# Threshold attention and a feed-forward layer on one core: v in wide packets, another key order, another order of work

## The chip, the cores and the metric

The kernel runs on one core of a Trainium2 chip. The metric is the time of one execution in device microseconds (us); less is better. A core has engines that each run their own list of instructions in order and wait for each other by semaphores: TensorE (PE in the profile, its weight loads PEld), VectorE (DVE), ScalarE (ACT), GpSimd (POOL) and SyncE (SP). SP only issues DMAs here; POOL issues DMAs and adds tensors. All DMAs run on the same 16 DMA engines.

## The reference

Eight batches of eight heads of attention over 576 positions with 64 dimensions per head, in which only scores within tau of their row's maximum count, and then a feed-forward layer with 512 model and 2048 hidden dimensions:

```
scores = (1/sqrt(64)) * q @ k.T
thresh = max(scores, axis=-1) - tau
scores = where(scores >= thresh, scores, -1e9)
scores = scores - max(scores, axis=-1)
attn   = exp(scores) / (sum(exp(scores)) + 1e-9)
x      = (attn @ v), heads side by side      # 4608 x 512
h      = x @ w_in
out    = (h * sigmoid(1.702 * h)) @ w_out
```

q, k and v are float32. The weights w_in and w_out come as float64, 16 pieces of 128 x 512 each, and the kernel turns them into float32 by operations on their bits.

## The kernel before

**Attention.** The work unit is a pair of heads; there are 32 pairs (n = 0 to 31), four per batch. A pair's keys are cut into nine tiles of 64. For every pair:

- `load_qk` (L366) and `load_v` (L377) issue the loads on SP, four DMAs for each of q, k and v; k of pair 0 alone goes by ACT's queue. q and k come in runs of 32 floats (128 B), v in runs of 64 (256 B). v stands twice in SBUF, once in each half of the partitions. Key number 64j + r lies in tile j, row r.
- `prep` (L477, VectorE) transposes q and k in blocks of 32; `scores` (L493, TensorE) makes the nine tiles of scores in PSUM; `keep` (L510, ACT) copies them to SBUF.
- `in_groups` (L516), `over_tiles` (L525), `over_halves` (L536, L542) and `turn_rows` (L553), all VectorE, find every query's maximum less the gap that tau gives. `row_out` (L566) writes this row of thresholds to DRAM and `row_in` (L575) reads it back to all partitions, both on SP. Pair 2 alone does without (`spread_max`, L557).
- `sub` (L580, VectorE) subtracts the row, `mask` (L586, ACT) sends what is below it to a huge negative number, `exps` (L590, ACT) takes exponentials. Each goes in five steps of two tiles, the last of one.
- `values` and `sums_by_pe` (both L601, TensorE; pv and den in the profile) multiply by v and by ones. From pair 5 on the sums are made on VectorE by `in_groups` with addition; pairs 5 to 7 then spread them by `one_group` and `spread_sums` (L643, L647, L684, L686), pairs from 8 on by `turn_sums` (L658 to L663) and a way through DRAM on SP (`sums_out` L668, `sums_in` L675).
- `place_x` (L703, VectorE) scales the product into the tiles xT. It frees the PSUM buffer of the product.

**Weights.** `load_w` (L428, L429, POOL) loads a piece by two DMAs of 512 KB into a staging place (six of them; a place is taken again when its piece is converted); `cv_ex` (L439), `cv_frac` (L453, L457), `cv_end` (L465) on VectorE and `cv_power` (L447) on ACT convert it. The task `hold` (L484, POOL) is a small copy that waits for a prepared k: weight loads 0 to 2 come after the k of pair 2, loads 3 to 5 after the k of pair 3. All later loads stand behind these in POOL's list.

**Feed-forward.** Two blocks of 256 rows are done plainly: `mm1_0` (L758), `tanh`, `gelu_0` (L764), `mm2` (L740), `half` (L747); the first step needs pairs 0 to 3 placed and w_in converted, `mm2` needs w_out converted. The blocks after them use sums of quarters of matrices so that seven products do the work of eight (L718, L909; for the last four blocks L823 too), with `t_minus` (L865, ACT) and `t_plus` (L869, POOL's DMA) making such sums of w_out once. POOL adds at L875 to L888.

**Start.** POOL sets a few constants (L944 to L947) and loads tau (L948). `tau_terms` (L960 to L969, VectorE) derives the gap from it; it comes after the preparing of pair 0's q and k and pair 1's q, and ahead of pair 1's k.

**What sets the order.** Nothing of this order is written out. The kernel describes each step as a task with an engine, a cost, the tasks it follows, buffers that it takes and gives back, and a rank: the pair's number plus a bias for the kind of step (tables `EARLY` for pairs 0 to 3, `SECOND` for pairs 4 to 7, `LATER`, and `CV` for the weights). `run_in_order` plays an event clock over these tasks while the program is built: whenever an engine is free it takes the ready task of lowest rank, and issues its instructions. So costs, lags (from the end of a task to when another engine may see it) and biases fix each engine's list, and the chip then runs the lists. A load was a task on SP with a fixed lag for its DMA (10.0 for q and k of pairs 4 to 7, 9.0 for a weight piece, 3.0 for v).

Of the kernel before, what the change touches and what calls it, by code (L numbers as in the profile page):

```python
# [19 lines left out]
P = 128  # L20
# [10 lines left out]
def kernel(  # L31
# [84 lines left out]
    stop = const.tile([P, 1], FP32, name="stop")  # L116
    shift = const.tile([P, 1], FP32, name="shift")
# [9 lines left out]
    for x in ("raw0", "raw1", "qkT0", "qkT1", "mb"):  # L127
# [6 lines left out]
        "exps": -11.47,  # L134
        "in_groups": 5.75,
        "keep": 10.66,
        "load_qk": -0.27,
        "load_v": 4.86,
        "mask": -2.66,
        "one_group": -15.86,  # L140
        "one_row": 12.67,
        "over_halves": -7.01,
        "over_tiles": -4.01,
        "place_x": -17.11,
        "prep": -11.73,
        "row_in": 20.49,
        "row_out": 4.47,
        "scores_run": 12.45,
        "spread_max": -1.73,
        "spread_sums": 7.14,  # L150
        "sub": 9.27,
        "sums_by_pe": 0.27,
        "sums_in": -9.39,
        "sums_out": 2.13,
        "turn_rows": -12.55,
        "turn_sums": -0.41,
        "values": 14.64,
        "w_sum": 4.11,
        "x_sum": -14.1,
    }  # L160
    SECOND = {
        "exps": -7.29,
        "in_groups": 20.95,
        "keep": 16.67,
        "load_qk": -8.88,
        "load_v": 5.53,
        "mask": 2.36,
        "one_group": 2.55,
        "one_row": -2.71,
        "over_halves": -12.07,  # L170
        "over_tiles": 2.86,
        "place_x": -20.26,
        "prep": 3.49,
        "row_in": -19.42,
        "row_out": -24.08,
        "scores_run": -7.99,
        "spread_max": -3.11,
        "spread_sums": -2.29,
        "sub": 14.98,
        "sums_by_pe": 35.93,  # L180
        "sums_in": 7.43,
        "sums_out": 4.05,
        "turn_rows": -3.84,
        "turn_sums": 4.03,
        "values": 11.79,
        "w_sum": -10.45,
        "x_sum": -10.98,
    }
    LATER = {
        "exps": 2.01,  # L190
        "in_groups": 10.37,
        "keep": -0.02,
        "load_qk": -6.6,
        "load_v": 3.77,
        "mask": 14.79,
        "one_group": 4.78,
        "one_row": -14.98,
        "over_halves": 1.09,
        "over_tiles": -6.27,
        "place_x": -0.34,  # L200
        "prep": 2.34,
        "row_in": 4.02,
        "row_out": 2.64,
        "scores_run": -11.25,
        "spread_max": -9.44,
        "spread_sums": -6.73,
        "sub": 2.14,
        "sums_by_pe": 1.46,
        "sums_in": 3.78,
        "sums_out": 2.16,  # L210
        "turn_rows": 12.26,
        "turn_sums": 0.29,
        "values": -10.38,
        "w_sum": 6.61,
        "x_sum": 6.02,
    }
    CV = {
        "cv_end": -8.05,
        "cv_ex": 2.22,
        "cv_frac": -11.72,  # L220
        "cv_power": -4.72,
        "load_w": -7.79,
    }

    LAG = {"PE": 0.26, "DVE": 0.18, "ACT": 0.22, "POOL": 0.18}

    QUARTERS = ("scores", "scores_run", "values", "sums_by_pe")
# [12 lines left out]
    FIRST, LAST = -9.0, 1000.0  # L240
    need, follows = {}, {}

    def run_in_order():
# [7 lines left out]
        events = [(0.0, 1, i) for i, n in enumerate(left) if n == 0]  # L251
# [3 lines left out]
        mode, held_for = None, None  # L255
        while events:
            now = events[0][0]
            while events and events[0][0] <= now:
                _, kind, i = heapq.heappop(events)
                engine, _, rank, _, _, _, _, give, lag = tasks[i]  # L260
                if kind == 0:
                    busy.discard(engine)
                    heapq.heappush(events, (now + lag, 2, i))
                elif kind == 1:
                    ready.setdefault(engine, []).append((rank, i))
                else:
                    for pool in give:
                        free[pool] += 1

                for u in users[i]:  # L270
                    if kind == (0 if tasks[u][0] == engine else 2):
                        left[u] -= 1
                        if left[u] == 0:
                            ready.setdefault(tasks[u][0], []).append((tasks[u][2], u))
            for engine, queue in ready.items():
                if engine in busy:
                    continue
                for rank, i in sorted(queue):
# [14 lines left out]
                cost = tasks[i][1]  # L293
                if engine == "PE":
# [3 lines left out]
                heapq.heappush(events, (now + cost, 0, i))  # L298
                started += 1
# [4 lines left out]
    JOINT = 7  # L304

# [53 lines left out]
    def load_qk(n, which, queue):  # L359
# [4 lines left out]
        for h in range(2):  # L364
            for j in range(2):
                queue.dma_start(  # L366
                    out=blocks[ds(64 * h + 32 * j, 32), :, :],
                    in_=src[b, 2 * hp + h, :, ts(j, 32)].rearrange("(c p) d -> p c d", p=32),
# [3 lines left out]
    def load_v(n):  # L372
        b, hp = divmod(n, NPAIR)
        t = seat("v_m", n % 2).rearrange("p (j h d) -> p j h d", j=NK, h=2)
        for h in range(2):
            for c in range(2):
                nc.sync.dma_start(  # L377
                    out=t[ts(c, KT), :, h, :],
                    in_=v[b, 2 * hp + h].rearrange("(j k) d -> k j d", k=KT),
# [109 lines left out]
    def scores(n, j):  # L489
# [8 lines left out]
        if j == NK - 1:  # L498
# [33 lines left out]
    def over_halves(n):  # L532
        r = stats[n, ALU.max]
        o = work.tile([P, QB], FP32, name="fold", tag="fold", bufs=1)
        for x in (1, 3) if n in BY_DMA else range(4):
# [3 lines left out]
            )  # L539
        if n in BY_DMA:  # L540
# [10 lines left out]
    def turn_rows(n):  # L551

        nc.vector.transpose(out=flat[1], in_=flat[0])  # L553

# [23 lines left out]
    def sub(n, t):  # L578
        s = sT[n, t].rearrange("p u h s -> p u (h s)")
        nc.vector.tensor_tensor(  # L580
# [26 lines left out]
    def values(n, tiles):  # L607
# [3 lines left out]
        by_values(n, lambda j, h: v_m[:, j, h, :], [pv[:, c, :] for c in range(2)], tiles)  # L611
        if n < NPAIR:
            free_scores(n, tiles)

    def sums_by_pe(n, tiles, apart):
# [9 lines left out]
        if not apart:  # L625
# [321 lines left out]
    nc.gpsimd.memset(ones, 1.0)  # L947
    nc.gpsimd.dma_start(  # L948
# [26 lines left out]
    BY_PE = 5  # L975
    BY_DMA = (0, 1, *range(3, NP))
    SUMS_BY_DMA = range(8, NP)
    LEAD = 6
    WHOLE = 6

    FFU = 1.727
    T_RANK = FIRST

    W_RANK = (0, 12.87, 12.51, 22.24, 0, 4.97)
    ready_w, w_loads, w64 = [], [], 0
    for i in range(len(pieces)):
# [10 lines left out]
        a = task("POOL", 1.1, rank, load_w, i, after=w_loads[-1:], take=place, lag=9.0)  # L997
        w_loads.append(a)
        e = task("DVE", 0.345, rank, cv_ex, i, after=[a])
        m = task("ACT", 0.67, rank, cv_power, i, after=[e])  # L1000
        a = task("DVE", 1.1, rank, cv_frac, i, after=[e])

        over = [ready_w[y] for y in range(i) if i >= n_in and stage(y) == (i - n_in) // PER_STAGE]
        ready_w.append(task("DVE", 0.61, rank, cv_end, i, after=[a, m] + over, give=place))
# [191 lines left out]
    for n in range(NP):  # L1196
# [5 lines left out]
        slow = 1.1 if n < NPAIR else 1.0  # L1202
# [3 lines left out]
        cost = 3.5 if NPAIR <= n < 2 * NPAIR else 2.0  # L1206
        lag = (4.6, 3.0)[n] if n < 2 else 10.0 if n < 2 * NPAIR else 3.0
        lq = task("SP", cost, r - 2.0, load_qk, n, 0, q0, after=behind, take=own(n, "raw0"), lag=lag)
        lk = task(
            "SP", cost if n else 0.1, r - 2.0, load_qk, n, 1, q1, after=behind,  # L1210
            take=own(n, "raw1"), lag=lag,
        )
        v_m = f"v_m{n % 2}"
        lv = task("SP", 2.4, r + (1.85 if n < 2 else -1.2), load_v, n, after=lvs[-1:], take=(v_m,), lag=3.0)
        lvs.append(lv)
        pq = task("DVE", 0.69, r, prep, n, 0, after=[lq], take=own(n, "qkT0"), give=own(n, "raw0"))
# [3 lines left out]
        if n in (2, 3):  # L1220
# [3 lines left out]
            for a in w_loads[3 * (n - 2) : 3 * (n - 1)]:  # L1224
# [3 lines left out]
        def copied(n, r, j, a):  # L1228
            copies.append(task("ACT", 0.55, r, keep, n, j, after=[a] + copies[-1:], give=("psA",)))
            if j % 2 or j == NK - 1:  # L1230
                mx.append(task(
                    "DVE", 1.27 if j % 2 else 0.66, r, in_groups, n, j // 2, ALU.max,
# [29 lines left out]
        else:  # L1262
            for js in [range(x, x + 3) for x in range(0, NK, 3)] if n >= WHOLE else [[x] for x in range(NK)]:
# [4 lines left out]
                    give=own(n, "qkT0", "qkT1") if js[-1] == NK - 1 else (),  # L1268
# [107 lines left out]
```

## Time and profile before

| what | us |
|---|---|
| median of 3 runs | 1317.7 |
| lowest, highest | 1315.8, 1318.82 |
| the profiled execution | 1317.94 |
| its span, first to last instruction | 1316.2 |
| PE busy in it | 1260.9 |
| DVE busy | 1006.1 |
| ACT busy | 646.6 |
| POOL busy | 249.0 |

The mean granted TensorE clock of the profiled run was 0.987. The profile names instructions by engine and line of the code; in a group's row, `out<-in` are the program's buffers. arena, w_out and w_in are the large SBUF tiles in which most small buffers have seats, so that the line says more than the name. Numbers in brackets at the end of a row in order of time are idle time of the engine before that group and what ended it. The page's slices cut the span into 40 equal parts and give the busy share in tenths.

### The profile page before, as it was taken

Reading aid. Unit: us, or ns where it says so; the run is one execution under the profiler, and the core shown is the slowest. Engines: PE = TensorE matmul, PEld = TensorE weight load, DVE = VectorE, ACT = ScalarE, POOL = GpSimd, SP = SyncE. Lnnn points to the kernel's source line nnn. Section 1 sums busy time; section 2 is a strip of 40 time slices with the busy share of each in tenths; the row PEclk is TensorE's granted clock in tenths of the full one; section 3 lists DMA queues with packets and bytes.
Section 4 is the critical chain, followed back from the end, with each engine's and each line's share of the span. In section 5 each row is a group of like instructions: output and inputs, shape, how many; then the busy total and the mean of one; then the engine's idle time right before and its main releaser. Section 6 shows DMA issues by size and latency. Waiting matters only on the chain. (4 is left out here: it accounts for less than half of the span.)

```text
span 1316.2 us, 22807 instructions
## 1 busy us (share of the span) xinstructions
PE 1260.9 (96%) x9128; PEld 975.6 (74%) x9128; DVE 1006.1 (76%) x1610; ACT 646.6 (49%) x830; POOL 249.0 (19%) x291
## 2 busy tenths in 40 slices
PE   5669999999999999999999999999999999999998
PEld 2346864457887777777778888777777778888887
DVE  7989999898888887788777877777888863652642
ACT  4876666576554555555554555454556540210210
POOL 1201211012031211213021303030212117120120
PEclk8879999999999999999999999999999999999999
DMA  8976766545323223212213222323122110000000
GB/s 152 293 189 207 230 207 149 112 77 100 85 55 71 55 55 71 51 50 54 58 42 72 55 71 55 71 55 71 36 55 54 36 46 8 9 1 25 8 0 32
DMA packets 258819, 102.88 MB, mean 78 GB/s; under 512 B 233754, under 2 KB 243994, under 8 KB 258714
## 3 DMA queue, kind: packets, MB, share of 16 engines
q1 hardware_dynamic: 244986, 63.40, 22.4%
q0 software_dynamic: 11360, 37.74, 9.3%
q8 instruction: 71, 1.16, 0.4%
q10 hardware_dynamic: 2368, 0.30, 0.2%
q14 instruction: 34, 0.28, 0.1%
HBM read 87.51 MB, written 9.69 MB: 74 GB/s over the span
## 5 line engine op out<-in xcount | busy, mean ns | idle before, releaser
L516 DVE TRANSPOSE_TENSOR_REDUCE part<-arena 128x36 f32<-128x1152 f32 (+1 forms) x295 | 357.5, 1235 | 41.9 <-ACT arena L510 32.4
L718 PE MATMUL hps<-xT,w_in 128*128 128x256 f32 x1536 | 337.2, 380 | 0.5 <-DVE arena L730 0.4
L718 PEld LDWEIGHTS hps<-xT,w_in 128*128 128x128 f32 x1536 | 290.7, 190 | 45.9 <-issue 5.7
L586 ACT ACTIVATE arena<-arena 128x1152 f32<-128x1152 f32 (+1 forms) x160 | 169.4, 1059 | 144.0 <-DVE arena L580 143.8
L510 ACT COPY arena<-ps 128x576 f32<-128x576 f32 x288 | 170.7, 647 | 115.3 <-PE ps L493 111.9
L580 DVE TENSOR_TENSOR arena<-arena 128x1152 f32<-128x1152 f32 (+1 forms) x158 | 201.1, 1313 | 20.5 <-DMA arena<-row 20.5
L909 PE MATMUL ops<-w_out,arena 128*128 128x256 f32 x896 | 202.4, 380 | 1.8 <-DVE arena L730 1.8
L590 ACT ACTIVATE arena<-arena,shift,scl 128x1152 f32<-128x1152 f32 (+1 forms) x160 | 200.3, 1252 | 4.1
L493 PE MATMUL ps<-arena 64*64 64x288 f32 x2304 | 174.7, 420 | 22.9 <-DVE arena L477 15.3
L909 PEld LDWEIGHTS ops<-w_out,arena 128*128 128x128 f32 x896 | 169.3, 190 | 28.7 <-DVE arena L730 3.1
L875 POOL TENSOR_TENSOR arena<-arena 128x256 f32<-128x256 f32 x56 | 49.7, 888 | 647.1 <-DVE arena L730 543.9
L601 PE MATMUL pv<-arena 64*64 64x288 f32 x2176 | 159.7, 408 | 0.0
L727 ACT ACTIVATE th<-hps 128x512 f32<-128x512 f32 x112 | 66.0, 589 | 186.0 <-PE hps L718 171.8
L909 PE MATMUL ops<-arena 128*128 128x256 f32 x672 | 150.7, 380 | 0.7 <-DVE osb L931 0.7
L493 PEld LDWEIGHTS ps<-arena 64*64 64x64 f32 x2304 | 84.0, 137 | 90.8 <-ACT arena L510 30.4
L909 PEld LDWEIGHTS ops<-arena 128*128 128x128 f32 x672 | 127.1, 190 | 20.4 <-issue 2.2
L601 PEld LDWEIGHTS pv<-arena 64*64 64x64 f32 x2176 | 82.1, 134 | 54.1 <-issue 10.0
L931 DVE SCALAR_TENSOR_TENSOR osb<-ops,osb 128x256 f32<-128x256 f32 x98 | 39.3, 413 | 97.9 <-PE ops L909 90.6
L730 DVE SCALAR_TENSOR_TENSOR arena<-th,hps 128x512 f32<-128x512 f32 x96 | 64.2, 669 | 46.7 <-ACT th L727 46.4
L740 PE MATMUL ops<-w_out,arena 128*128 128x512 f32 x128 | 57.2, 600 | 3.2 <-DVE w_out L465 2.2
L758 PE MATMUL hps<-xT,w_in 128*128 128x256 f32 x256 | 56.4, 381 | 0.0
L888 POOL TENSOR_TENSOR arena<-arena 128x512 f32<-128x512 f32 x28 | 35.6, 1272 | 108.3 <-PE ops L909 108.3
(115 smaller groups left out, 1044.7 us busy)
## 6 DMA issues: line engine op xcount, KB each, us to landing
arena<-in_v_dram SPq DMA_DIRECT2D x128, 144.0 KB
arena<-in_q_dram SPq DMA_DIRECT2D x128, 72.0 KB
out_dram<-osb SPq DMA_DIRECT2D x36, 256.0 KB
arena<-in_k_dram SPq DMA_DIRECT2D x124, 72.0 KB
arena<-row SPq DMA_DIRECT2D x62, 144.0 KB
arena<-row_s SPq DMA_DIRECT2D x48, 144.0 KB
w_out<-in_moe_w_in_dram POOLq DMA_DIRECT2D x12, 512.0 KB, 9.5
arena<-in_moe_w_out_dram POOLq DMA_DIRECT2D x12, 512.0 KB, 6.3
```

The costliest lines, as they stand in the source:

```text
L493: nc.tensor.matmul(ps[ts(c, KT), h, 0:SH], lhsT=mats[n, 1][ts(h, D), ts(j, KT)], rhs=mats[n, 0][ts(h, D), ts(c, SH)], start=True, stop=True,)
L510: nc.scalar.copy(out=sT[n, t][:, u], in_=pss.pop((n, j))[:, :, 0:SH])
L516: nc.vector.tensor_reduce(out=stats[n, op][:, t * 2 * QB : min(2 * t + 2, NK) * QB], in_=sT[n, t].rearrange("p u h (g d) -> p (u h g) d", ...
L580: nc.vector.tensor_tensor(out=s, in0=s, in1=mbs[n].unsqueeze(1).to_broadcast(list(s.shape)), op=ALU.subtract)
L586: nc.scalar.activation(out=s, in_=s, func=AF.Prelu, alpha=STEEP)
L590: nc.scalar.activation(out=s, in_=s, func=AF.Exp, scale=scl, bias=shift)
L601: nc.tensor.matmul(o[c][ts(h, D), 0:SH], lhsT=left(j, h)[ts(c, KT)], rhs=sT[n, t][ts(c, KT), u, h, :], start=(j == 0), stop=(j == NK - 1),)
L718: nc.tensor.matmul(hidden[j][:, ts(f, BLK)], lhsT=w_in[:, c, ds((f * HF + j) * P, P)], rhs=xTs[blk][:, c, :], start=(c == 0), stop=(c == N ...
L727: nc.scalar.activation(out=ths[j], in_=hidden[j], func=AF.Tanh, scale=GELU_SCALE / 2)
L730: nc.vector.scalar_tensor_tensor(out=g[:, :, j, :], in0=two(ths.pop(j)), scalar=1.0, in1=two(hidden.pop(j)), op0=ALU.add, op1=ALU.mult,)
L740: nc.tensor.matmul(acc[i], lhsT=g0[:, j, ts(i, P)], rhs=w_out[:, j, :], start=(j == 0), stop=(j == NFC - 1),)
L909: nc.tensor.matmul(banks[blk][k][:, ts(o, HM)], lhsT=left[:, j, :], rhs=right[:, j, :], start=(j == 0), stop=(j == HF - 1),)
```

## The change

- **v.** A partition takes nine consecutive keys of a head, 9 x 64 floats in one run of 2304 B; key 9r + j lies in tile j, row r. The k loads are reordered to match: the same 128 B runs from other rows. Where v is used, two indices change places.
- **Planner.** A load becomes two tasks: the issue on its queue (SP or POOL), and a transfer on one of two movers, DMS for SP's loads and DMW for weights. Alone a mover runs at full rate; together SP's transfer gets a share of 0.055 (packets of 128 B) or 0.3 (others), the weights the rest. Costs of SP's issues and of some VectorE and ACT steps have new figures.
- **Biases.** All values of the four tables but one or two and the ranks of the weight pieces (`W_RANK`) change, so the order on every engine does.
- **Weights.** The first six loads all come after the k of pair 3.
- **Sums.** Pairs 5 to 7 turn their sums by DMA too (`SUMS_BY_DMA` from 5 on). The condition under which the seats of the scores are given back is written in terms of the new list `SUMS_BY_PE`.
- **Start.** POOL sets two more constants, `minus` and `own_row`, ahead of tau's load. They serve functions (`row_blocks`, `again`, `mask_one`) for pairs in `TWICE`, and `BY_POOL` would move some subtractions to POOL; both lists are empty, so none of this is issued.

The diff, cut to its core:

```diff
+    minus = const.tile([P, 2, KT], FP32, name="minus")
+    own_row = const.tile([P, QB // 2], FP32, name="own_row")
...
     EARLY = {
-        "exps": -11.47,
-        "in_groups": 5.75,
+        "exps": -17.61,
+        "in_groups": 12.77,
...
+    MOVERS = ("DMS", "DMW")
+    SHARE = (0.055, 0.3)
+    def transfer(by, time, a, kind=0, give=(), lag=1.7):
+        return task(by, time, FIRST, moved, kind, after=[a], give=give, lag=lag)
...
+        def rates():
+            if len(flow) < 2:
+                return dict.fromkeys(flow, 1.0)
+            x = SHARE[tasks[flow["DMS"][0]][4][0]]
+            return {"DMS": x, "DMW": 1.0 - x}
...
+    TWICE = ()
+    BY_POOL = {}
...
+                rows = src[b, 2 * hp + h, :, ts(j, 32)]
                 queue.dma_start(
                     out=blocks[ds(64 * h + 32 * j, 32), :, :],
-                    in_=src[b, 2 * hp + h, :, ts(j, 32)].rearrange("(c p) d -> p c d", p=32),
+                    in_=rows.rearrange("(a p t) d -> p t a d", a=2, p=32) if which
+                    else rows.rearrange("(c p) d -> p c d", p=32),
                 )
...
-        t = seat("v_m", n % 2).rearrange("p (j h d) -> p j h d", j=NK, h=2)
+        t = seat("v_m", n % 2).rearrange("p (h j d) -> p h j d", j=NK, h=2)
         for h in range(2):
             for c in range(2):
                 nc.sync.dma_start(
-                    out=t[ts(c, KT), :, h, :],
-                    in_=v[b, 2 * hp + h].rearrange("(j k) d -> k j d", k=KT),
+                    out=t[ts(c, KT), h],
+                    in_=v[b, 2 * hp + h].rearrange("(k j) d -> k j d", k=KT),
                 )
...
-        by_values(n, lambda j, h: v_m[:, j, h, :], [pv[:, c, :] for c in range(2)], tiles)
+        by_values(n, lambda j, h: v_m[:, h, j, :], [pv[:, c, :] for c in range(2)], tiles)
...
     nc.gpsimd.memset(ones, 1.0)
+    nc.gpsimd.memset(minus, 0.0)
+    nc.gpsimd.memset(own_row, 0.0)
+    for x in range(4):
+        nc.gpsimd.memset(minus[ts(x, 32), x % 2, :], -1.0)
+        nc.gpsimd.affine_select(
+            out=own_row[ts(x, 32)], in_=own_row[ts(x, 32)], compare_op=ALU.not_equal, fill=1.0,
+            base=-(QB // 2) * (x // 2), pattern=[[-1, QB // 2]], channel_multiplier=1,
+        )
     nc.gpsimd.dma_start(
         out=tau_b, in_=bass.AP(tensor=tau.tensor, offset=tau.offset, ap=[[0, P], [1, 1]])
     )
...
-    BY_PE = 5
+    SUMS_BY_PE = (0, 1, 2, 3, 4)
     BY_DMA = (0, 1, *range(3, NP))
-    SUMS_BY_DMA = range(8, NP)
+    SUMS_BY_DMA = range(5, NP)
...
-    W_RANK = (0, 12.87, 12.51, 22.24, 0, 4.97)
+    W_RANK = (0, 15.75, 22.55, 26.06, 2.06, 16.74)
...
-        a = task("POOL", 1.1, rank, load_w, i, after=w_loads[-1:], take=place, lag=9.0)
+        a = task("POOL", 1.1, rank, load_w, i, after=w_loads[-1:], take=place)
         w_loads.append(a)
+        a = transfer("DMW", 3.4, a)
...
-        cost = 3.5 if NPAIR <= n < 2 * NPAIR else 2.0
-        lag = (4.6, 3.0)[n] if n < 2 else 10.0 if n < 2 * NPAIR else 3.0
-        lq = task("SP", cost, r - 2.0, load_qk, n, 0, q0, after=behind, take=own(n, "raw0"), lag=lag)
+        cost = (2.6, 2.4, 2.9, 2.4)[n] if n < NPAIR else 2.1
+        lq = task("SP", cost, r - 2.0, load_qk, n, 0, q0, after=behind, take=own(n, "raw0"))
...
+        lq, lk = (transfer("DMS", 1.45, a, lag=1.7 if n else 3.0) for a in (lq, lk))
...
-        lv = task("SP", 2.4, r + (1.85 if n < 2 else -1.2), load_v, n, after=lvs[-1:], take=(v_m,), lag=3.0)
+        lv = task("SP", 3.0, r + (1.85 if n < 2 else -1.2), load_v, n, after=lvs[-1:], take=(v_m,))
         lvs.append(lv)
+        lv = transfer("DMS", 1.1, lv, 1)
...
-        if n in (2, 3):
+        if n == 3:
             h = task("POOL", 0.3, FIRST, hold, n, after=[pk])
-            for a in w_loads[3 * (n - 2) : 3 * (n - 1)]:
+            for a in w_loads[0:6]:
                 tasks[a][5].append(h)
```

## The prediction

> **What bounds the kernel now.** I read the page's slices first, then busy time in stretches of 10 us, then what VectorE (DVE), TensorE (PE), SyncE (SP) and GpSimd (POOL) did in order of time, with the wait before each group in brackets. The slices:
>
> ```profile
> PE   5669999999999999999999999999999999999998
> DVE  7989999898888887788777877777888863652642
> ```
>
> A slice is 32.9 us. From the fifth on TensorE is full: there the time is its own work, which the change leaves alone (4566 matmuls in both programs). Only its idle time can go: span 1316.2 less 1260.9 busy is 55.3 us. The first 120 us hold 41.2 of them, 180 to 330 us 7.2, and 3.4 lie after the last matmul.
>
> ```profile
> 20.00:30.00 10.00, 4.03 (x40) 2.49 (x44) 9.83 (x16) 2.77 (x6) 3.52 (x8) 0.66 0.72 157
> 70.00:80.00 10.00, 0.76 (x12) 0.21 (x8) 9.80 (x14) 7.05 (x7) 0.00 (x0) 0.69 1.13 316
> 110.00:120.00 10.00, 9.52 (x132) 5.71 (x124) 9.24 (x22) 7.71 (x13) 0.00 (x0) 1.00 0.70 226
> 120.00:130.00 10.00, 10.00 (x51) 8.66 (x47) 9.83 (x13) 3.15 (x5) 3.17 (x6) 1.00 0.57 210
> ```
>
> Third column PE, then weight loads, then DVE: while TensorE has 4.0 or 0.8 of 10 us, VectorE has 9.8. The first 115 us are VectorE's: softmax work of four pairs and the conversion of w_in. TensorE fills up once pair 3 (the fourth) is placed and the feed-forward layer can start:
>
> ```profile
> 9.16 0.11 DVE L960 TENSOR_SCALAR neg<-tau_b 128x1 f32<-128x1 f32 x1
> 34.67 2.63 DVE L580 TENSOR_TENSOR arena<-arena 128x1152 f32<-128x1152 f32 x2 [0.23 <-DMA arena<-row]
> 88.56 2.63 DVE L580 TENSOR_TENSOR arena<-arena 128x1152 f32<-128x1152 f32 x2 [3.70 <-DMA arena<-row]
> 114.40 0.95 DVE L703 TENSOR_TENSOR xT<-pv,arena 128x256 f32<-128x256 f32 x4
> ```
> ```profile
> 117.60 1.99 PE L758 MATMUL hps<-xT,w_in 128*128 128x256 f32 x8
> 215.38 20.01 PE L740 MATMUL ops<-w_out,arena 128*128 128x512 f32 x46 [1.63 <-DVE w_out L465]
> 271.23 1.78 PE L493 MATMUL ps<-arena 64*64 64x288 f32 x16 [2.16 <-ACT arena L510]
> ```
>
> So the time is VectorE's until pair 3 is placed, then TensorE's plus a few waits. The gates: row DMAs, and the two chains that the edits at the start touch:
>
> ```profile
> 26.20 1.13 SPq L575 DMA_DIRECT2D arena<-row  x2
> ```
> ```profile
> 1.39 0.75 POOL L948 DMA_DIRECT2D tau_b<-in_tau_dram  x1 [0.35 <-issue]
> 25.89 0.18 POOL L484 COPY stop<-arena 128x1 f32<-128x1 f32 x1 [23.75 <-DVE arena L477]
> 26.01 0.56 POOL L428 DMA_DIRECT2D w_out<-in_moe_w_in_dram  x1
> ```
> ```profile
> L875 POOLq MODIFY_POOL_CONFIG  x2: 675/675/675, 284.1 to 284.1; - x2
> ```
>
> **What the Trainium skill says.** GPSIMD Engine Reference, 2.1 Instruction dispatch: the first call into a freshly loaded library pays a load of about 6 us (5.95) that the profile doesn't show. Here POOL's first tensor op comes at 290.10, 6.0 after the load instruction at 284.1, but VectorE released it only at 290.02: the trace bounds the price from above, no more. DMA: Bandwidth & Descriptors, Queues, rings and completion order: an engine goes round its queues by whole packets. The trace agrees: between 72 and 73 us, under weight loads, SP's queue moved 88 small packets, between 80 and 81 alone 1140. The same page, Specifications, asks for 512 B or more per transfer: those 1140 packets were 0.14 MB, against 0.42 MB in the weights' microsecond.
>
> **Part by part.** Sums are made against the profiled run (1317.94; span 1316.2 and 1.74 around it); the median of the runs is 1317.7, 0.2 less.
>
> *v in packets of 2304 B, keys reordered.* A pair's v was 2304 packets of 256 B; it becomes 256. At about 1013 packets/us (5066 in 10 to 15 us) 2.3 us of all DMA engines become 0.59 MB at 0.35 MB/us, 1.7. k keeps 128 B packets in another order. No wait on v is in the list of waits, so the path gains nothing: 0, cover being that v comes microseconds ahead of the values matmul. SP's issue of a v load (0.63 each, L377) is between the 0.48 of the like-shaped row load (L575) and the planner's new 0.75: four of them 0.6 less or 0.5 more, beside VectorE work.
>
> *New order up to pair 3.* In the built program I compared VectorE's lists up to the last place_x of pair 3. They hold the same work but for one more cv_end (0.61). Before, that point ended at 115.35. Of the waits between 19.46 (pair 0's row turned) and there, 6.0 in all, the list shows 0.23 and 3.70 on row DMAs, 0.80 on ACT's power, 0.97 on scores that held a transpose's target. The 3.70 came from SP: pair 3's row was ready at 77.8 but sent at 82.19, behind v3, q4 and k4. In the new list q4 and k4 are through by about 66 (v3 waits for pair 1's values at about 59, then 2.7 and 4.3), the row goes at 80.4 on time, and between its turn and its first use VectorE has pair 2's placing and three conversions: 8.6 us, against 7.3 for v4's issue (2.7), row_out (0.7), row_in (1.1) and landing (2.6, from 85.98 to 88.56), and 0.2 between. Also the two q/k prepares stand late enough. So 115.35 + 0.61 - 6.0 = 110.0, plus new waits:
> - Pair 1's row. SP sends it when VectorE has turned it (30.3), takes it in 33.0 to 34.1; before, row 0 issued to 27.3 beside three weight pieces was used at 34.67 (7.3 later). 41.4 against a use at 40.7 to 41.0: 0.4.
> - Conversion power: ACT has pair 4's nine copies ahead of pieces 5 to 7: 0.9.
> - tau, below: 3.0.
>
> Placed at 114.3. Then TensorE has still to end pair 5's scores, which ACT copies at about 0.8 each behind five powers: 1.4 later, 115.7. Before it began at 117.60 with 0.5 of those scores undone, so 118.1. **First part: -2.4.**
>
> *First six loads behind k of pair 3.* They start when that k is prepared: 31.0 by the sum, not 25.9. Queued behind POOL's copy are all loads, nothing else; VectorE's conversions wait for them. Piece 0's second DMA landed about 8.1 after the start (the tenth DMA, waiting for it, went at 34.16): 39.2, use at 39.6. 0, with no margin; in return row 0 travels without weights beside it.
>
> *POOL's added constants.* Two memsets, four pairs of memset and affine_select, and a library load before the first select stand ahead of tau's DMA; behind that DMA wait tau_terms and, in order on VectorE, everything from pair 1's k on. Memsets to 1.5 (0.10 to 0.15 each, 0.74 on), load instruction 0.7, the page's 5.95, seven ops at about 0.15: 9.2; landing 3.9: 13.1. VectorE wanted tau at 9.16 and had 0.94 of waits just after, so 3.0. Low end 0 (load hidden); high end 6 (DMA engines are at 104% between 10 and 15 us). I take 3.0. The rest of these constants feeds branches with empty lists.
>
> *Pairs 5 to 7 turn sums by DMA.* Per pair four fold copies stay; out go 0.69 (L647), 0.27 and 0.78, in come 0.18, 0.27, 0.21: 1.1 less, 3 in all, on a VectorE that TensorE waits for only in the next item; on SP four DMAs more per pair (about 1.9), between 200 and 260 us where it stands waiting anyway. 0 by itself. The freeing of score seats is the same at its moment; the planner's costs act only through the order.
>
> *New order after the start of the feed-forward layer.* Up to the last conversion of w_out VectorE's list holds 183 us of work, before 199 (each kind times its mean): sums and maxima of pairs 5 to 7 now stand behind it. So it ends near 195 where it ended at 215.32, and TensorE needs it near 198. That removes 1.63 and 0.60. The 2.16 before L493 (ACT was in pair 7's exponentials) goes too: pair 7's subtractions are done some 15 us before TensorE gets there. Left are about 0.9 of GELU waits, 0.9 where ACT's two sign copies stand between score copies, 0.5 others: 2.3 of the 7.2. That is 4.9; I take **-3.5**, since the old order met waits too that its list alone doesn't show. After 330 us: 0.
>
> Sum: 1317.9 - 2.4 - 3.5 = **1312.0**.
>
> **Rivals.** *A, as summed:* 1312, own range 1308 to 1315. For it: VectorE's 9.8 of 10. *B, tau isn't late:* the first part is 5.4 and the second up to 4.9: 1317.9 - 9.9 = 1308. For it: the trace never shows the load's price; against: the page. *C, given back:* the second part is spent on waits that the list doesn't show (row 5, q7 under the last loads): 1317.9 - 2.4 + 1 = 1316.5. Speaks for it: q and k crawl under weights (88 against 1140 packets). *D, slower: pair 1's row drowns in six loads released in its own microsecond.* Before, three pieces went ahead; now twelve DMAs of 0.5 MB at 0.35 MB/us flow 17 us, from 35 to 52. If row_in lands only with them, VectorE stands at pair 1's first sub (43.7, tau included) for 8.5 us with everything behind it. 6.1 more than cancel 5.9, and the second part shrinks by half as TensorE catches less: 1312 + 8.5 + 1.8 = 1322. It decides from a wait of 6 us. Against it: round-robin gave row 0 its 0.3 MB in 6.5 us. *That the packets don't do what they say* gives A: nothing waits on v.
>
> **Chances.** A 0.50, B 0.22, C 0.16, D 0.12. Measured apart can be about 0.2%, 2.6 us: faster is below 1315.1. That is nearly all of A (0.49), B, and 0.04 of C: 0.75; same 0.12 of C, 0.01 of A and 0.02 of D: 0.15; slower 0.10. Range 1305 to 1320: it takes in B's low end and C, and leaves out most of D and B with every wait gone.
>
> **What would show it.** Right: tau_terms near 13; L666's first sub on pair 0 near 34, before any conversion; hps begins near 115.7; last L510 near 195; no wait on w_out at ops. Wrong: a wait of several us before pair 1's sub (D), tau near 9 (B), hps no earlier than 117.6 or waits on hps and ps above 7 us between 180 and 330 (C).

## The result and the profile after

| what | before | after |
|---|---|---|
| median, us | 1317.7 | 1312.81 |
| lowest, highest | 1315.8, 1320.58 | 1311.6, 1315.22 |
| profiled execution | 1317.94 | 1311.6 |
| its span | 1316.2 | 1309.8 |
| PE busy in it | 1260.9 | 1260.5 |

The ratio of after to before is 0.9962, with an interval of 0.9948 to 0.9975: 4.9 us faster, against 1312.0 forecast. TensorE's work is as it was; its idle time went from 55.3 to 49.3 us. The profiled execution of after is its quickest, so the two profiles lie 6.3 us apart where the medians lie 4.9 apart.

The page's slices after:

```profile
PE   5869999999999999999999999999999999999998
DVE  7999998989998877778877877777888864652642
```

TensorE's second slice rises from 6 to 8, and its long row of nines stays. Where the idle time went shows in busy time by stretch. The third column is PE, then weight loads, DVE, ACT, POOL, the granted clock, the share of the DMA engines and GB/s. First before, then after:

```profile
0.00:120.00 120.00, 79.00 (x1016) 45.33 (x1016) 103.53 (x179) 87.16 (x110) 18.74 (x43) 0.87 0.81 208
120.00:180.00 60.00, 60.00 (x400) 49.15 (x396) 58.44 (x99) 30.74 (x39) 13.39 (x24) 1.00 0.74 238
180.00:240.00 60.00, 55.91 (x371) 27.75 (x373) 58.34 (x98) 41.12 (x54) 7.42 (x10) 1.00 0.66 151
240.00:330.00 90.00, 86.90 (x697) 54.64 (x690) 80.30 (x120) 60.82 (x77) 13.10 (x14) 0.98 0.49 93
```
```profile
0.00:120.00 120.00, 82.32 (x1036) 46.09 (x1037) 107.88 (x186) 88.57 (x113) 20.89 (x52) 0.90 0.75 208
120.00:180.00 60.00, 58.74 (x381) 47.19 (x383) 56.83 (x102) 28.29 (x38) 15.59 (x28) 1.00 0.84 270
180.00:240.00 60.00, 59.66 (x319) 28.02 (x312) 54.47 (x76) 44.40 (x52) 5.45 (x6) 1.00 0.67 139
240.00:330.00 90.00, 86.17 (x746) 58.12 (x744) 81.66 (x125) 58.64 (x76) 17.87 (x16) 0.98 0.44 90
```

In the first stretch TensorE gains 3.3 us. From 120 to 330 its idle time goes from 7.2 to 5.4 us (1.26 + 0.34 + 3.83): 3.75 better between 180 and 240, but 1.26 and 0.7 given back on either side. After 330 it is 0.9 less: a single wait of 1.42 for a GELU, at 1094.93 before, is gone, and one of 1.10, at 670.48 after, is new.

VectorE in order of time, after:

```profile
9.25 0.11 DVE L1054 TENSOR_SCALAR neg<-tau_b 128x1 f32<-128x1 f32 x1
11.04 0.78 DVE L522 STREAM_TRANSPOSE arena<-arena 128x576 f32<-128x576 f32 x1 [0.99 <-DMA arena<-in_k_dram]
30.98 5.79 DVE L666 TENSOR_TENSOR arena<-arena 128x1152 f32<-128x1152 f32 x5
40.97 2.62 DVE L666 TENSOR_TENSOR arena<-arena 128x1152 f32<-128x1152 f32 x2
109.26 0.95 DVE L789 TENSOR_TENSOR xT<-pv,arena 128x256 f32<-128x256 f32 x4
```

`tau_terms` (first row) starts at 9.25 with no wait, as before. The row waits are gone: row 0's subtractions start at 30.98, row 1's at 40.97, neither with a bracket, and pair 3's 3.70 us has no successor. New is a wait for pair 1's k, but it costs nothing: before, VectorE waited 0.94 us for score copies just after that point (0.40 and 0.54), and these waits are gone. Pair 0's row is turned at 19.47, where it was turned at 19.46. Pair 3 is placed at 110.2, not 115.35. TensorE after:

```profile
110.27 3.73 PE L538 MATMUL ps<-arena 64*64 64x288 f32 x32 [1.64 <-DVE xT L789]
113.93 26.25 PE L844 MATMUL hps<-xT,w_in 128*128 128x256 f32 x120
246.30 1.43 PE L538 MATMUL ps<-arena 64*64 64x288 f32 x16 [2.44 <-ACT arena L555]
```

The feed-forward layer (hps) begins 3.7 us earlier than before. The waits for w_out are gone, but a wait for score copies of the same size as the old 2.16 stands at 246.30. GpSimd at the start:

```profile
1.44 0.19 POOL L1038 TENSOR_SCALAR_AFFINE_SELECT own_row<-own_row 32x9 f32<-32x9 f32 x1
2.85 0.75 POOL L1042 DMA_DIRECT2D tau_b<-in_tau_dram  x1
31.22 1.13 POOL L529 COPY stop<-arena 128x1 f32<-128x1 f32 x1 [27.62 <-DVE arena L522]
```
```profile
L1038 POOLq MODIFY_POOL_CONFIG  x2: 11/11/11, 1.3 to 1.4; - x2
```

The selects run 0.19 us each straight after load instructions of 11 ns, where the one at 284.1 before took 675. tau is issued at 2.85 and used on time.

### The profile page after: what moved, and what is told of

It reads as the page before. It is cut to its first block, busy times and chain, and to the rows that moved or that the text cites. A ratio compares the mean times of both kernels' runs of the same rounds, so it can differ in the third digit from the quotient of the medians.

```text
span 1309.8 us, 22824 instructions
## 1 busy us (share of the span) xinstructions
PE 1260.5 (96%) x9128; PEld 972.6 (74%) x9128; DVE 1002.2 (77%) x1601; ACT 646.6 (49%) x830; POOL 246.1 (19%) x300
## 5 line engine op out<-in xcount | busy, mean ns | idle before, releaser
L561 DVE TRANSPOSE_TENSOR_REDUCE part<-arena 128x36 f32<-128x1152 f32 x295 | 361.5, 1241 | 45.9 <-ACT arena L555 32.3
L804 PEld LDWEIGHTS hps<-xT,w_in 128*128 128x128 f32 x1536 | 290.8, 190 | 45.5 <-issue 5.7
L666 DVE TENSOR_TENSOR arena<-arena 128x1152 f32<-128x1152 f32 (+1 forms) x158 | 197.5, 1281 | 19.6 <-DMA arena<-row 19.5
L687 PEld LDWEIGHTS pv<-arena 64*64 64x64 f32 x2176 | 82.0, 135 | 55.3 <-issue 12.8
L844 PEld LDWEIGHTS hps<-xT,w_in 128*128 128x128 f32 x256 | 48.1, 190 | 11.0 <-DVE arena L850 3.0
```

What stands on the lines that cost most here:

```text
L561: nc.vector.tensor_reduce(out=stats[n, op][:, t * 2 * QB : min(2 * t + 2, NK) * QB], in_=sT[n, t].rearrange("p u h (g d) -> p (u h g) d", ...
L666: engine.tensor_tensor(out=s, in0=s, in1=mbs[n].unsqueeze(1).to_broadcast(list(s.shape)), op=ALU.subtract)
L687: nc.tensor.matmul(o[c][ts(h, D), 0:SH], lhsT=left(j, h)[ts(c, KT)], rhs=sT[n, t][ts(c, KT), u, h, :], start=(j == 0), stop=(j == NK - 1),)
L804: nc.tensor.matmul(hidden[j][:, ts(f, BLK)], lhsT=w_in[:, c, ds((f * HF + j) * P, P)], rhs=xTs[blk][:, c, :], start=(c == 0), stop=(c == N ...
L844: nc.tensor.matmul(hidden[j][:, ts(i, BLK)], lhsT=w_in[:, c, ts(j, P)], rhs=xTs[i][:, c, :], start=(c == 0), stop=(c == NDC - 1),)
```

## The experiments

A ratio is always to the kernel before. A difference of two ratios is turned into us with 1317.7; each ratio has an interval of about 0.001 to 0.0016 either way, 1.3 to 2 us, so a difference of two is known to some 2 to 3 us. One profiled execution can lie up to 5 us from the median of its kernel. A place in a trace is read to a microsecond or two: the kernel after and experiments 1, 8 and 9 have the same work for VectorE up to pair 3, and place that pair at 110.2, 110.7, 112.3 and 111.6. My theory after the result: what comes earlier on VectorE up to pair 3 comes earlier at the end, one for one. Its rival: the gain is the second part's, and the first has cover.

**1. No constants.** The two memsets and the loop of memsets and selects ahead of tau's load are taken out of the kernel after; nothing reads them.

```
-    nc.gpsimd.memset(minus, 0.0)
-    nc.gpsimd.memset(own_row, 0.0)
-    for x in range(4): ...
```

> The changed kernel without the two new constants of GpSimd (minus and own_row, ten operations and a library load ahead of tau's load); nothing reads them, every other engine's list is the same. The prediction's step (tau 3.0 us late through the library load): 1312.8 - 3 = about 1310, first tau_terms unchanged at 9.2 and all of VectorE's list some 3 us earlier. Theory from the trace after (selects of 0.19 us each, tau there at 7.1 for a use at 9.25, so no wait): 1312.8, within 1.5, tau's load issued near 1.4 instead of 2.85 and tau_terms still near 9.2.

Ratio 0.9954 (0.9939 to 0.997), 1311.83 us. The added constants cost nothing that can be seen.

**2. tau late.** The loop runs 17 times in place of 4, so that tau really is late.

```
-    for x in range(4):
+    for x in [0, 1, 2, 3] * 4 + [0]:
```

> The kernel after with 13 more rounds of a memset and a select ahead of tau's load on GpSimd, 5.5 us, so that tau lands near 12.6 us and VectorE waits about 3 us for it, as the prediction took. The prediction's step says that all of it reaches the end of the first part: +3.0, 1315.8 (ratio 0.9985). The rival: VectorE makes it good where it waits or has work in reserve (0.99 us for pair 1's k falls away, the six weight pieces are early), +0 to +1.5, 1312.8 to 1314.3.

Ratio 0.9979 (0.9969 to 0.9988), 1315.44 us: 2.2 us more than after. VectorE in order of time in this kernel:

```profile
12.57 0.15 DVE L1054 TENSOR_SCALAR neg<-tau_b 128x1 f32<-128x1 f32 x1 [3.33 <-DMA tau_b<-in_tau_dram]
111.99 0.95 DVE L789 TENSOR_TENSOR xT<-pv,arena 128x256 f32<-128x256 f32 x4
```

The wait is 3.33, and the 0.99 for pair 1's k disappears in it: 2.3 us net, 2.2 at the end. As far as an uncertainty of 2 us lets one say, such a delay has no cover.

**3. The packets and the key order on the old lists.** The kernel before with v's packets and the key order of the change, all else as it was.

```
-                    in_=src[b, 2 * hp + h, :, ts(j, 32)].rearrange("(c p) d -> p c d", p=32),
+                    in_=rows.rearrange("(a p t) d -> p t a d", a=2, p=32) if which else ...
...
-                    in_=v[b, 2 * hp + h].rearrange("(j k) d -> k j d", k=KT),
+                    in_=v[b, 2 * hp + h].rearrange("(k j) d -> k j d", k=KT),
```

> The kernel before with only the v packets of 2304 B and the reordered k loads; all lists as before. Theory that the order carries the gain: 1317.7, within 2, no wait on v before or after; k's issue on SP 0.65 us each instead of 0.50 as in the trace after, which may cost up to 1 us where pair 1's k is waited for. Rival, the packets carry the gain (the DMA engines freed early let rows and q/k land sooner): 1313 to 1315, and VectorE's waits of 0.23 and 3.70 us on the row DMAs gone or halved.

Ratio 1.0024 (1.0014 to 1.0034), 1321.11 us: 3.2 slower than before, which neither theory foresaw. The profiled execution took 1325.99; most of what it lies above the median is one wait of 4.63 for a GELU at 309.68, far behind the part read here. VectorE's new waits in it, and SP ahead of them:

```profile
11.22 0.78 DVE L479 STREAM_TRANSPOSE arena<-arena 128x576 f32<-128x576 f32 x1 [1.20 <-DMA arena<-in_k_dram]
37.06 2.63 DVE L582 TENSOR_TENSOR arena<-arena 128x1152 f32<-128x1152 f32 x2 [1.48 <-DMA arena<-row]
```
```profile
19.75 2.68 SPq L367 DMA_DIRECT2D arena<-in_k_dram  x4
22.47 2.57 SPq L379 DMA_DIRECT2D arena<-in_v_dram  x4
25.14 0.81 SPq L568 DMA_DIRECT2D row<-flat  x2
```

The second number of an SP row is the time of its issues. Four of k take 2.68 where they took 2.06 before: the median of one issue of k is 652 ns, against 497 before. SP works without a gap up to row 0, so three such loads send the row at 25.14, not 23.50.

**4. v's packets alone on the old lists.** As 3, with k read in its old order, so that the kernel leaves out what keeps a value with its key.

```
-                    in_=rows.rearrange("(a p t) d -> p t a d", a=2, p=32) if which
-                    else rows.rearrange("(c p) d -> p c d", p=32),
+                    in_=rows.rearrange("(c p) d -> p c d", p=32),
```

> The kernel before with v in packets of nine keys alone, k as it was, so that a value no longer belongs to its key. With both, it took 3 us more than before. If that came from the key order (k's issue, the waits of 1.2 us for pair 1's k and 1.5 us for row 0), this gives 1316 to 1318 (ratio 0.999 to 1.000) with pair 3 placed near 115. If it came from v's packets, it stays at 1321 (1.002), placed near 117.5.

Ratio 0.9997 (0.9981 to 1.0013), 1318.51 us. k's issue is 497 ns again, row 0's wait is gone and row 0 leaves at 23.08. So on the old lists v's packets are worth nothing that can be seen, and the key order costs 3.6 us (1.0024 less 0.9997).

**5. The new order with the old packets.** Experiment 1's kernel with v and k loaded as before.

> The changed kernel with v in 256 B packets and k in the old order again, and without the two constants; VectorE's, ScalarE's and TensorE's lists are those of the changed kernel. Theory that the order carries the gain: 1312.8, within 2. Rival, the packets carry it: back to 1316 to 1318, with VectorE waiting for q/k or the rows of pairs 0 to 3.

Ratio 0.9986 (0.9972 to 1.0), 1316.64 us: 4.2 more than the same kernel with the new packets (experiment 1), as the rival had it. SP from 45 us in this kernel, then in the kernel after:

```profile
45.35 24.27 SPq L420 DMA_DIRECT2D arena<-in_v_dram  x8
69.67 6.11 SPq L409 DMA_DIRECT2D arena<-in_q_dram  x4
75.83 2.12 SPq L409 DMA_DIRECT2D arena<-in_k_dram  x4
```
```profile
45.67 15.65 SPq L422 DMA_DIRECT2D arena<-in_v_dram  x8
61.38 8.70 SPq L410 DMA_DIRECT2D arena<-in_q_dram  x4
70.13 6.16 SPq L410 DMA_DIRECT2D arena<-in_k_dram  x4
```

The issues stretch while weights flow beside them: at 9 us, without weights, eight such issues took 5.5 us in small packets and 5.1 in large ones. v of pairs 2 and 3 holds SP for 24.3 us in small packets, 15.7 in large ones, and pair 4's q is through at 75.8, not 70.1. VectorE in the kernel with the old packets waits for that q, for k, and then for ScalarE's part of a conversion, a wait that is only 0.23 in the kernel after:

```profile
77.86 0.78 DVE L520 STREAM_TRANSPOSE arena<-arena 128x576 f32<-128x576 f32 x1 [0.86 <-DMA arena<-in_q_dram]
80.06 0.78 DVE L520 STREAM_TRANSPOSE arena<-arena 128x576 f32<-128x576 f32 x1 [0.76 <-DMA arena<-in_k_dram]
91.20 0.69 DVE L508 SCALAR_TENSOR_TENSOR w_in<-arena 128x512 f32<-128x512 int32 x1 [1.45 <-ACT arena L490]
```

Pair 3 is placed at 113.3, against 110.7 in experiment 1: some 2.6 of the 4.2. The rest lies behind it, where in these two traces VectorE's waits for weight pieces between 112 and 200 us come to 8.3 in place of 5.0, and TensorE's for GELUs of the first blocks to 3.6 in place of 1.5. So the packets seem to help the weights as well as q; no run takes the two apart. On the old lists the same saving bought nothing: in experiment 4 v holds SP 17.6 us in place of 22.9, but q and k behind it then take 12.7 in place of 7.5, and k is through at 81.6 against 82.1. There pair 3's row stood behind that k; in the new order it doesn't, and q's arrival counts.

**6. k in its old order in the kernel after.** The edit of experiment 4, on the new lists.

> The kernel after with v in packets of nine keys and k read in its old order with three dimensions, so that a value no longer belongs to its key: only the time of the loads is asked for. If the key order's dearer issue (0.65 us against 0.50) costs what the prediction left out, k's issue falls to 0.50, VectorE's wait of 0.99 us for pair 1's k falls to about 0.2, pair 3 is placed up to 0.8 us earlier, near 109.5, and the time falls by as much, to 1312.0. If it was covered, 1312.8.

Ratio 0.9968 (0.9957 to 0.9978), 1313.98 us. VectorE in this kernel:

```profile
10.47 0.78 DVE L521 STREAM_TRANSPOSE arena<-arena 128x576 f32<-128x576 f32 x1 [0.34 <-DMA arena<-in_k_dram]
13.34 1.38 DVE L560 TRANSPOSE_TENSOR_REDUCE part<-arena 128x36 f32<-128x1152 f32 x1 [0.54 <-ACT arena L554]
15.19 3.30 DVE L560 TRANSPOSE_TENSOR_REDUCE part<-arena 128x36 f32<-128x1152 f32 x3 [0.48 <-ACT arena L554]
```

The wait for pair 1's k is 0.34 in place of 0.99, but waits for score copies stand behind it in this execution; pair 3 is placed no earlier (111.5), and the time isn't lower. In the new order the key order costs nothing that can be seen. The way of row 0 out to DRAM goes ahead of pair 3's k, its way back has no weights beside it, and VectorE wants it only at 31.

**7. Three loads early.** The first three weight loads behind k of pair 2, as before, the other three behind k of pair 3; the engines' lists are those of after.

```
+        nc.gpsimd.tensor_copy(out=stop, in_=held_k[2][:, 0:1])
+        for i in range(3):
+            load_w(i)
         nc.gpsimd.tensor_copy(out=stop, in_=held_k[n][:, 0:1])
...
```

> The changed kernel, but the first three weight loads go behind the k of pair 2 and only the next three behind the k of pair 3, as before; other engines' lists the same. Theory that the later start is what keeps row 0 free: loads start near 25 instead of 32, row 0 (issued 26.3 to 27.6) lands near 34 as it did before, the first subtraction starts at 34 instead of 31, and 3 us pass to the end: 1315 to 1316. Rival, as the prediction's zero for this part: the loads' start doesn't matter, 1312.8 within 1.5, subtraction at 31.

Ratio 0.9993 (0.9981 to 1.0006), 1317.87 us: 4.1 more than after, and more than the 3 expected. GpSimd, SP and VectorE in this kernel:

```profile
25.72 0.57 POOL L473 DMA_DIRECT2D w_out<-in_moe_w_in_dram  x1 [0.31 <-issue]
```
```profile
26.16 1.24 SPq L667 DMA_DIRECT2D arena<-row  x2
```
```profile
35.76 5.83 DVE L673 TENSOR_TENSOR arena<-arena 128x1152 f32<-128x1152 f32 x5 [4.15 <-DMA arena<-row]
113.96 0.95 DVE L796 TENSOR_TENSOR xT<-pv,arena 128x256 f32<-128x256 f32 x4
```

Row 0 is issued at 26.16 to 27.40, in the company of loads that began at 25.72, and lands at 35.8. SP in the kernel after:

```profile
26.34 1.24 SPq L660 DMA_DIRECT2D arena<-row  x2
```

There it is issued at 26.34 to 27.58 and is there by 30.98, when VectorE takes it without a wait. The old order has 5.1 us of maxima ahead of that use, which hid most of row 0's way (0.23 of a wait was left); the new one hasn't. So in the new order the loads' later start alone is worth 4.1 us.

**8. The sums of pairs 5 to 7 on VectorE**, as before, in the lists of after: one_group where turn_sums stood, spread_sums just ahead of place_x, the row_s transfers left out.

> The kernel after with the sums of pairs 5 to 7 formed and spread on VectorE as before (one_group where turn_sums stood, spread_sums ahead of place_x), every other instruction in its place. The prediction's step says 0 by itself: 1312.0 to 1313.6. The rival: 1.1 us more on VectorE for each of three pairs, between 220 and 330 us where TensorE has 3.8 us of waits left, +1 to +3, 1314 to 1316 (ratio 0.997 to 0.9985).

Ratio 0.9958 (0.9943 to 0.9973), 1312.63 us. No difference.

**9. Only the second part late.** 18 small transposes on VectorE behind place_x of pair 3: TensorE gets its x at the same time, and VectorE's later list is pushed back.

```
+        for _ in range(18 if n == 3 else 0):
+            nc.vector.transpose(out=flat_s[1], in_=flat_s[0])
```

> The kernel after with 18 small transposes (some 3 us) on VectorE just behind place_x of pair 3, so that TensorE gets its x at the same time and only VectorE's later list is pushed back. If the second part is still set by VectorE's list, as the prediction's step on w_out has it, with 2.3 us or less in reserve, the time rises by 1 to 3 us, to 1314 to 1316. If the order after leaves the conversions waiting for weight pieces (3.7 us of VectorE's waits for them between 112 and 200 us), those waits shrink and little is seen: 0 to +1.

Ratio 0.9991 (0.9981 to 1.0002), 1317.61 us: 3.8 more than after. Of the two theories the second falls: the waits for weight pieces do not absorb the delay, they even come to 5.4 in place of 3.7. The delay in this kernel, TensorE's waits between 112 and 330 us in it, and the same waits in the kernel after:

```profile
111.54 4.39 DVE L794 STREAM_TRANSPOSE flat_s<-flat_s 128x32 f32<-128x32 f32 x18
```
```profile
PE ps L538 <- ACT arena L555: 4.2, 2, 3.2
PE hps L846 <- DVE arena L852: 3.3, 7, 1.0
```
```profile
PE ps L538 <- ACT arena L555: 3.7, 3, 2.4
PE hps L844 <- DVE arena L850: 1.2, 3, 0.8
```

Columns are us in total, times, the longest. The transposes took 4.4 and not the 3 expected, and that delay costs 3.8: the second part is still VectorE's. It shows not at w_out but at the GELUs of the first blocks (hps waiting for L852: 1.2 becomes 3.3) and at score copies. This bears on experiments 2 and 7 too. Their delays push back all of VectorE's list, the later part with the first, and the later part alone passes on nearly all of a delay. So what is shown is that the list as a whole has hardly any cover; that the first part alone has none isn't shown apart. The traces speak for it: TensorE's waits for score copies and GELUs between 112 and 330 us, 5.3 after, did not shrink clearly behind a later start of hps (6.3 in experiment 2, 4.6 in 7).

**10. Pair 1's k on ScalarE's queue**, in search of a quicker version: ScalarE has nothing to do until 10 us, and SP would be free 2.9 us earlier.

```
-        q0, q1 = (nc.sync, nc.scalar) if n == 0 else (nc.sync, nc.sync)
+        q0, q1 = (nc.sync, nc.scalar) if n < 2 else (nc.sync, nc.sync)
```

> The kernel after with the k of pair 1 issued on ScalarE's queue behind the k of pair 0, in place of SP's. ScalarE has nothing to do until 10 us, so its four issues (2.8 us) are hidden, and SP reaches v, pair 2 and the rows 2.9 us earlier. If what delays pair 3's x passes on to the end one for one, the 0.99 us wait for pair 1's k goes, pair 3 is placed near 109.3, and the time falls by about 1 us, to 1311.8 (ratio 0.9955). If the wait has cover, or the earlier loads crowd pair 1's q, nothing: 1312.8 or a little more.

Ratio 0.9968 (0.9959 to 0.9978), 1314.65 us: no gain. VectorE in this kernel:

```profile
9.91 0.78 DVE L522 STREAM_TRANSPOSE arena<-arena 128x576 f32<-128x576 f32 x1 [0.91 <-DMA arena<-in_q_dram]
12.20 0.78 DVE L522 STREAM_TRANSPOSE arena<-arena 128x576 f32<-128x576 f32 x1 [0.79 <-DMA arena<-in_v_dram]
```

The wait moved to pair 1's q and stayed with k. The name v in the bracket is that of the DMA that came last by the profile; this transpose reads k. The issues themselves stretched: SP's first eight of q took 7.02 us in place of 5.20, so SP reached v only 0.95 us earlier (8.02 for 8.97), and ScalarE was through with pair 1's k at 8.4, where SP had been at 8.9. That more packets met at the DMA engines fits (their share from 8 to 16 us is 0.88 in place of 0.78), but isn't shown apart.

**11. k with three dimensions**, on the kernel after and on the old lists, to bring k's issue down with v's packets kept.

```
-                    in_=rows.rearrange("(a p t) d -> p t a d", a=2, p=32) if which
+                    in_=rows.rearrange("(p c) d -> p c d", p=32) if which
...
-                    in_=v[b, 2 * hp + h].rearrange("(k j) d -> k j d", k=KT),
+                    in_=v[b, 2 * hp + h].rearrange("(p a j) d -> a p (j d)", a=2, p=32),
...
```

> The kernel after with the same keys beside each other, but in a key order that lets k be read with three dimensions in place of four: row 32a + p of tile j holds key 18p + 9a + j, v's partitions follow it in packets of nine keys, and the VectorE transpose of k reads its blocks in another order. If the dearer issue of k (0.65 us in the kernel after against 0.50 before, four times a pair) is what holds VectorE 0.99 us for pair 1's k, k's issue falls to about 0.50, that wait to 0.1 to 0.3, and the time by 0 to 1 us, to 1312 to 1313 (ratio 0.9955 to 0.9965). If k's cost is in its transfers and not in the issue, nothing changes: 1312.8, the wait stays. If the reordered transpose is slower than 0.78 us, it costs its difference in the first part.

> The kernel before with v in packets of nine keys and the key order that lets k be read with three dimensions. With four dimensions these packets made the kernel before slower by 3 us (ratio 1.0024), with pair 1's k waited for 1.2 us and row 0 for 1.5 us. If k's dearer issue was the cause, this gives 1317 to 1318 (ratio 0.999 to 1.000), and those waits fall back to 0 and 0.2. If the packets themselves harm the old order, it stays at 1321 (1.002).

Ratios 1.1738 (1.1714 to 1.1762) and 1.1454 (1.1426 to 1.1482), 1549.21 and 1510.87 us. Both expectations fall, above all for a reason that lies in neither theory: v. SP in the first of them, and its busy time from 8 to 25 us (next to last column the DMA engines' share, then GB/s):

```profile
8.72 15.10 SPq L422 DMA_DIRECT2D arena<-in_v_dram  x8
23.95 11.61 SPq L410 DMA_DIRECT2D arena<-in_q_dram  x4
```
```profile
8.00:25.00 17.00, 12.39 (x144) 5.57 (x144) 11.47 (x21) 10.35 (x18) 0.00 (x0) 0.99 0.21 54
```

The kernel after has a DMA share of 0.68 and 137 GB/s in that stretch. v's source now begins with a dimension of 2. The Trainium skill, DMA: Bandwidth & Descriptors, Why a DMA increments its semaphore by 16 and not by 1, says that the slowest dimension sets how many of the 16 engines a transfer uses; the trace agrees: from 10 to 23 us, while SP issued nothing but v, the share is 0.14, and two of 16 would be 0.125. The drop expected in k's issue didn't come either: with three dimensions its median is 630 ns on SP in both kernels, not 500. So most of what the new key order's issue costs more isn't due to the fourth dimension; what it is due to stays open.

## Why the prediction was right, step by step

The total (4.9 us gained for 5.9 forecast) came out of steps of which several were off and cancelled, so that its closeness is in part luck.

**First part, -2.4: too small; it was about -3.7, or -4.2 in the step's own measure, from 118.1 to 113.9.** The step "of the waits ... 6.0 in all" held: they went. Of the new waits, tau (3.0) and pair 1's row (0.4) did not come, and conversion power (0.9) came as 0.23; 0.22 for the first weight piece is new. So pair 3 was placed at 110.2 and not 114.3, close to the step's 110.0 without any new wait. In it q4 and k4 were through by about 66; k4 was through at 76.3, since v stretched under the weights, and that was still early enough for pair 3's row at 80.7. The term "1.4 later" for pair 5's scores was too small the other way: hps began 3.7 after the placing. Four tiles had waited for the placing to end; here they took 3.73, at a granted clock of 0.59 between 110 and 114 us. In experiment 1 the same 32 matmuls took 2.19 at a clock of 1.00. With the scatter of single executions (hps begins at 112.9 to 115.3 in the kernel after and experiments 1, 8 and 9) the first part is known to 1 or 2 us. The price that the step put on a delay, one for one, fits: net delays of 2.3 us (experiment 2) and 4.15 (7) cost 2.2 and 4.1, each known to some 2 us.

**"tau, below: 3.0": the premise failed, the price held.** The Trainium skill, GPSIMD Engine Reference, 2.1 Instruction dispatch, has 5.95 us for the first call into a freshly loaded kernel. No such load stood before these selects: 1.44 is their start, 11 ns the load instruction. The trace of before left everything from 0 to 6 open, and I took the page's figure, though no profile had shown that this operation calls freshly loaded code. Taking 3.0 out of the forecast alone would have given 1309, too low: rival B in its cause, but not in its time.

**"First six loads behind k of pair 3 ... 0": wrong as a part.** I priced what the weights lose by starting later, of which only 0.22 for the first piece showed up to pair 3, and mentioned in half a sentence that row 0 travels alone. That was the part's value: 4.1 us in the new order (experiment 7). It was inside the sum all the same, because the 6.0 us of waits were counted as gone. Parts that only pay together can't be given a zero one by one: order without packets 0.9986 (there without the constants, which cost nothing), packets without order 1.0024, both 0.9962. Read the other way, the order is worth 8.2 us with the new packets, of which the loads' start is 4.1, and 1.8 with the old.

**"v in packets ... 0" and k's order at nothing: each is true in one order only.** On the old lists v's packets are worth 0 within 2 us (experiment 4) and the key order costs 3.6 us. On the new ones the packets with their key order are worth 4.2 (experiments 1 and 5) and the key order costs nothing (6). The step looked for a wait on v. What v holds up is SP, and with it q; in the trace of experiment 5 weight pieces come later too. That k's issue would take 0.65 us in place of 0.50 it didn't foresee.

**Pairs 5 to 7, 0 by itself:** right (experiment 8).

**Second part, -3.5: smaller.** Its sum was itself off by a little: of the waits from 180 to 330 us it lists as left, one of 0.43 at 311.25 is missing, so that 4.4 and not 4.9 would have gone. From the start of hps to the end of the profiled execution it is 1200.3 us before and 1197.7 after: -2.6, of which -1.8 of TensorE's idle time lies in 120 to 330 us and about -0.9 after it, where the step said 0. The last w_out conversion came at 196.8 to 197.5 (195 forecast, 215.32 before), and no matmul waited for w_out: right. That "the 2.16 before L493 goes too" was wrong: 2.44 of the same kind stands at 246.30. And GELU waits came to 1.2. VectorE also waited 3.7 us for weight pieces between 112 and 200, where it had waited for none before. How much of the 4.9 belongs to the second part stays open: over the eight kernels whose lists are those of after (experiment 8's but for three sums), that distance is 1197.7 to 1203.2 in their single profiled executions, against 1198.9 to 1206.2 in three with the old lists, and the two ranges overlap.

**The rivals.** C was right in that new waits would come, not in their size. D, pair 1's row drowned, did not happen; but experiment 7 shows that the mechanism is real and a microsecond away: row 0 started 0.4 us behind the weights and landed 8.4 us after its last issue, and with the loads held back it was there within 3.4 us. Pair 1's row in the kernel after did travel among the weights: issued until 33.4, it was still moving on SP's queue after 39 us, and VectorE took it at 40.97.

## What to carry to other kernels

Where one engine sets the pace up to a point, price a part of a change by what it does to that engine's waits in the new order, not in the old: the same packets with their key order cost 3.2 us in one order and gained 4.2 in the other. A small transfer that a busy engine waits for should be away before bulk loads start: here a start of theirs 6.6 us later was worth 4.1. A price that no trace of the kernel shows is a bound, and the likelier value needs a reason of its own.

## What was new about the hardware

- Reading the same 128 B runs of k in another key order raised the issue on SP from 497 to 652 ns (median of 124), and on ScalarE's queue from 516 to 678 (median of four). The fourth dimension of the source is at most a small part of it: an order read with three took 630 and 653 (experiment 11).
- v in 2304 B runs under weights held SP's queue 15.7 us for eight loads, against 24.3 in 256 B runs (experiment 5).
- A transfer whose source begins with a dimension of 2 drew the DMA share down: 0.14 while SP issued nothing else, from 10 to 23 us, where the kernel after has 0.72 (experiment 11).
- The same kind of load instruction on GpSimd (MODIFY_POOL_CONFIG) took 11 ns ahead of the selects and 675 ahead of the first tensor add of the kernel before.
